# When the loads of B21, x and chunk 1 run, and in how many pieces, in a GEGLU feed-forward kernel (with the A22 copies split)

## The chip, the cores and the metric

One core of one Trainium2 chip. The metric is the device time of the kernel in microseconds (us). The kernel before the change takes 541.47 us, the median of three runs (540.5 to 542.04).

## The reference

```python
B, S, D, F = 1, 2048, 1024, 3584      # all in bfloat16
def reference(x, w_gate, w_up, w_down):
    return (gelu_tanh(x @ w_gate) * (x @ w_up)) @ w_down
```

## The kernel before

The kernel works on two halves of the sequence. In each half the gate and up projections are done in pairs of columns, and then the down projection in two groups, so there are four down groups in all (0 to 3). Every block product uses a scheme of seven products, M1 to M7, in place of eight; their operands are sums such as S1 to S4 (of the activations) and T1 to T4 (of the weights). T2 and T4 of the down projection are prepared in advance by VectorE ("staging", from pair 2 of the first half on), stored in device memory (`t_dram`), and loaded back for each group. SP issues nearly all loads and stores, in program order.

The loads of the down groups:

```python
def load_b21(n, q):                  # B21 of W_down, in 4 pieces of some 512 KB
    ...                              # pieces 0 to 2 into wd_sb buffers, the last into o_sb
    sp(nc.sync.dma_start(out=w[:, 0 : i1 - i0, :], in_=src))
    b21_tiles[(n, q)] = w

def t_down(grp, name, i0, i1):
    for i in range(i0, i1, 2):
        ...
        if name in ("t2", "t4"):
            src = t_dram[:, 0 if name == "t2" else 1, i : i + 2, :]
            sp(nc.sync.dma_start(out=t.bitcast(F32), in_=src))
        ...
```

One down group, cut to what the change touches:

```python
product("m5", VB, lsum(0), rsum("t1"), True, False, behind_m5)   # first of T2's loads in here
...
def behind_m6(i):
    ...
    if i == 4:
        for q in range(4):
            load_b21(n, q)
product("m6", QB, lsum(0), rsum("t2"), False, False, behind_m6, tail)
...
done("m6")                           # here the x loads (group 0) or chunk loads (group 1) are issued
product("m7", RB, lsum3, rsum("t3"), False, False, behind_m7, head)   # first of T4's loads in here
...
s_down(hT, grp, "a22", 0, NS)        # 7 copies on ScalarE, needed by M4
out22 = evacuate(VB, 1, 1)
done("m7")
store(out22)
product("m2", PB, h_block(0, 1), b21, False, True)
...
product("m3", QB, lsum(0), rsum("b22"), False, True, behind_m3)
...
product("m4", RB, lsum(1), rsum("t4"), False, True, behind_m4, tail)
```

The staging step, which the change does not touch but which the result turns on:

```python
def stage_step(n):                   # three subtractions for each block of W_down
    ...
    dve(nc.vector.tensor_tensor(out=t, in0=in0, in1=in1, op=ALU.subtract))
    if k > 0:
        sp(nc.sync.dma_start(out=t_dram[:, k - 1, i, :], in_=t.bitcast(F32)))
...
if h == 0 and pair >= PPG:           # PPG is 2: from pair 2 on; two steps in it, four in the next
    n = [min(max(4 * (pair - PPG + d) - 2, 0), NSTEP) for d in range(3)]
    steps = [lambda k=k: stage_step(k) for k in range(n[0], n[1])]
    new = range((n[1] + 2) // 3, (n[2] + 2) // 3)
```

The fill of the second half, during groups 0 and 1:

```python
def x_fill(k0, k1):
    src = x_dram[:, k0:k1, :]
    sp(nc.sync.dma_start(out=xT[0][:, k0:k1, :], in_=src))

def w_fill(c, j):
    if j == 0:
        new_chunk((nh, c))
    for k0 in range(0, KD, KH):      # two halves of each weight chunk
        load_w((nh, c), j, k0, k0 + KH)

then0["m6"] = [lambda k0=k0: x_fill(k0, k0 + WKP) for k0 in range(0, KD, WKP)]   # 4 loads
```

## Time and profile before

| | kernel before |
|---|---|
| time, median of 3 | 541.47 us (540.5 to 542.04) |
| the profiled run | 541.16 us, span 539.3 us |
| TensorE busy | 99% of the span |
| last matmul's start to the end of the span | 3.91 us |

The span is what the profile covers of one execution. TensorE is idle for 5.2 us of it (539.3 less 534.1), the start and the end included, so little is to be won by removing waits. The prediction shows the lines that locate one of them.

### The profile page before, as it was taken

To read this page: it belongs to the slowest core of one execution; us is meant where nothing else is said; L and a number is where in the kernel's file an instruction comes from. 1 tells how busy PE (TensorE), PEld (TensorE's weight loads), DVE (VectorE), ACT (ScalarE), POOL (GpSimd) and SP (SyncE) were. 2 spreads that over 40 slices of the span, in tenths; PEclk is the share of its full clock that TensorE was granted. 3 is DMA by queue.
4 is the path that set the end of the run, shared out by engine and by line. 5 is a ranking of instruction groups with operands and counts; after the bars stand their busy time and mean duration, and the time that the engine had idled before them with its cause. 6 is when DMAs were issued, how large, how long until landed. Compare 5 with 4: busy or idle time off the path is not lost.

```text
span 539.3 us, 7115 instructions
## 1 busy us (share of the span) xinstructions
PE 534.1 (99%) x2384; PEld 377.3 (70%) x2384; DVE 362.5 (67%) x478; ACT 263.2 (49%) x446; POOL 235.3 (44%) x208
## 2 busy tenths in 40 slices
PE   8999999999999999999999999999999999999997
PEld 3577776676776686767776767777777766866865
DVE  1968776887877997989574334444444469969951
ACT  2545555555555329117465555555555551552270
POOL 1069877777777000000056776666777730000000
PEclk9999999999999999999999999999999999999999
DMA  9954877695826977789950504042231466677846
GB/s 215 290 169 108 282 208 231 211 278 158 272 86 229 354 248 241 238 277 305 324 176 1 156 1 157 15 142 63 93 115 42 157 192 230 226 245 237 290 147 207
DMA packets 84836, 102.70 MB, mean 190 GB/s; under 512 B 18752, under 2 KB 66368, under 8 KB 84800
## 3 DMA queue, kind: packets, MB, share of 16 engines
q1 hardware_dynamic: 62400, 80.49, 47.1%
q10 hardware_dynamic: 22400, 21.76, 13.0%
q8 instruction: 19, 0.31, 0.2%
q14 instruction: 17, 0.14, 0.1%
HBM read 85.98 MB, written 12.58 MB: 183 GB/s over the span
## 4 chain that ended last, share of the span: by engine, by line
PE 97%; DMA 2%; ACT 0%; DVE 0%; issue 0%; ACTq 0%
PE bank L391 63%; PE bank L672 31%; PE bank L255 3%; DMA t_mem<-t_dram 1%; DMA w_mem<-in_x_dram 1%; PE bank L306 0%; ACT o_sb L725 0%; DVE xT L314 0%; ACTq L725 0%
## 5 line engine op out<-in xcount | busy, mean ns | idle before, releaser
L391 PE MATMUL bank<-t_mem,s_mem 128*128 128x512 f32 x1056 | 249.6, 394 | 0.0
L391 PEld LDWEIGHTS bank<-t_mem,s_mem 128*128 128x128 f32 x1056 | 198.1, 188 | 44.1 <-DVE bank L414 0.6
L362 POOL TENSOR_TENSOR s_mem<-w_mem 128x512 fp32r<-128x512 bf16 x102 | 117.4, 1171 | 200.5 <-DMA w_mem<-in_w_up_dram 102.7
L672 PE MATMUL bank<-t_mem,s_mem 128*128 128x512 f32 x544 | 127.4, 393 | 0.1
L279 DVE TENSOR_TENSOR hT<-w_mem,bank 128x512 bf16<-128x512 f32 x104 | 71.2, 687 | 82.9 <-PE bank L391 42.7
L672 PEld LDWEIGHTS bank<-t_mem,s_mem 128*128 128x128 f32 x544 | 102.1, 188 | 22.6 <-issue 0.5
L414 DVE TENSOR_TENSOR bank<-bank,m 128x512 f32<-128x512 f32 x108 | 69.9, 694 | 48.0 <-ACT m L439 44.0
L391 PE MATMUL bank<-xT,w_mem 128*128 128x512 bf16 x432 | 98.1, 380 | 0.0
L274 ACT ACTIVATE w_mem<-bank 128x512 f32<-128x512 f32 x104 | 61.8, 597 | 54.0 <-DVE bank L414 35.4
L391 PEld LDWEIGHTS <-w_mem 128*128 128x128 bf16 x432 | 40.2, 98 | 51.6 <-issue 6.8
L582 DVE TENSOR_TENSOR t_mem<-w_mem 128x1024 fp32r<-128x1024 bf16 x56 | 65.6, 1219 | 0.0
L362 POOL TENSOR_TENSOR s_mem<-w_mem,s_mem 128x512 fp32r<-128x512 bf16 x50 | 62.8, 1277 | 0.0
L362 POOL TENSOR_TENSOR s_mem<-s_mem,w_mem 128x512 fp32r<-128x512 f32 x50 | 57.4, 1167 | 0.0
L444 ACT COPY bank<-bank 128x512 f32<-128x512 f32 x54 | 30.8, 570 | 38.9 <-PE bank L391 37.2
L375 ACT CAST s_mem<-w_mem 128x512 fp32r<-128x512 bf16 x54 | 33.1, 615 | 31.7 <-PE bank L391 29.2
L647 DVE TENSOR_TENSOR s_mem<-hT 128x512 fp32r<-128x512 bf16 x52 | 34.2, 687 | 10.1 <-PE bank L672 9.4
L439 ACT COPY m<-bank 128x512 f32<-128x512 f32 x54 | 31.8, 589 | 18.4 <-PE bank L391 18.0
L672 PEld LDWEIGHTS <-hT 128*128 128x128 bf16 x224 | 21.2, 98 | 26.7 <-issue 2.1
L449 ACT COPY bank<-bank 128x512 f32<-128x512 f32 x54 | 30.7, 570 | 12.2 <-PE bank L391 12.2
L725 ACT CAST o_sb<-bank 128x512 bf16<-128x512 f32 x28 | 15.4, 585 | 40.0 <-PE bank L672 40.0
L607 DVE TENSOR_TENSOR o_sb<-wd_sb,o_sb 128x512 fp32r<-128x512 bf16 x28 | 30.4, 1085 | 0.5
L579 ACT CAST t_mem<-w_mem 128x1024 fp32r<-128x1024 bf16 x28 | 26.9, 1047 | 0.0
(45 smaller groups left out, 237.4 us busy)
## 6 DMA issues: line engine op xcount, KB each, us to landing
t_mem<-t_dram SPq DMA_DIRECT2D x56, 512.0 KB, 5.4
w_mem<-in_w_gate_dram ACTq DMA_DIRECT2D x10, 1024.0 KB, 5.5
w_mem<-in_w_up_dram ACTq DMA_DIRECT2D x10, 1024.0 KB, 8.2
wd_sb<-in_w_down_dram SPq DMA_DIRECT2D x28, 256.0 KB, 4.8
t_dram<-o_sb SPq DMA_DIRECT2D x28, 256.0 KB, 2.4
wd_sb<-in_w_down_dram SPq DMA_DIRECT2D x12, 512.0 KB, 8.1
w_mem<-in_w_down_dram SPq DMA_DIRECT2D x10, 512.0 KB, 7.5
w_mem<-in_w_down_dram SPq DMA_DIRECT2D x4, 1024.0 KB, 6.5
```

The costliest lines, as they stand in the source:

```text
L274: act(nc.scalar.activation(out=g_sb, in_=ps[:], func=ACT.Gelu_apprx_tanh))
L279: nc.vector.tensor_tensor(out=hT[:, fc, tb * TB : (tb + 1) * TB], in0=g_sb, in1=ps[:], op=ALU.mult,)
L362: pool(nc.gpsimd.tensor_tensor(out=t, in0=in0, in1=in1, op=op))
L375: act(nc.scalar.copy(out=t, in_=a(1, 1)))
L391: nc.tensor.matmul(banks[bank][:], lhsT=lhs[:, c, :], rhs=rhs[:, c, :], start=start and c == 0, stop=c == KH - 1, skip_group_check=True,)
L414: nc.vector.tensor_tensor(out=banks[dst][:], in0=banks[src][:], in1=m5[j][:], op=ALU.add)
L439: act(nc.scalar.copy(out=m5[j][:], in_=banks[V_[j]][:]))
L444: act(nc.scalar.copy(out=banks[RB[j]][:], in_=banks[QB[j]][:]))
L449: act(nc.scalar.copy(out=banks[QB[j]][:], in_=banks[P_[j]][:]))
L582: dve(nc.vector.tensor_tensor(out=t, in0=in0, in1=in1, op=ALU.subtract))
L647: dve(nc.vector.tensor_tensor(out=t, in0=in0, in1=in1, op=op))
L672: nc.tensor.matmul(banks[bset[u]][:], lhsT=lhs(i, u), rhs=rhs(i), start=start and i == 0, stop=stop and i == NS - 1, skip_group_check=True,)
```

## The change

Its intent: keep B21 from crowding the last loads of T2, move x out of the way of the T4 loads, issue fewer and larger loads, and let the output casts of M7 start before all seven A22 copies are done. The order of instructions on TensorE is the same in both kernels. (`t_loads`, kept in lines cut here, lists the T2 and T4 loads in order of issue, so `t_loads[-2]` is the sixth of the seven T2 loads.)

```diff
     def load_b21(n, q):
...
-        sp(nc.sync.dma_start(out=w[:, 0 : i1 - i0, :], in_=src))
+        load = nc.sync.dma_start(out=w[:, 0 : i1 - i0, :], in_=src)
+        if q == 0:
+            t2 = t_loads[-2]
+            tc.add_manual_dep(load.ins, t2.ins.name, SYNC_DEP, reason="rate")
+        sp(load)
...
-            if i == 4:
-                for q in range(4):
-                    load_b21(n, q)
-
+        for q in range(2):
+            load_b21(n, q)
+        done("b21")
+        for q in range(2, 4):
+            load_b21(n, q)
         product("m6", QB, lsum(0), rsum("t2"), False, False, behind_m6, tail)
...
-        s_down(hT, grp, "a22", 0, NS)
+        s_down(hT, grp, "a22", 0, NT2)
         out22 = evacuate(VB, 1, 1)
+        s_down(hT, grp, "a22", NT2, NS)
...
-            def x_fill(k0, k1):
-                src = x_dram[:, k0:k1, :]
-                sp(nc.sync.dma_start(out=xT[0][:, k0:k1, :], in_=src))
+            def x_fill():
+                sp(nc.sync.dma_start(out=xT[0][:], in_=x_dram[:]))
...
-                for k0 in range(0, KD, KH):
-                    load_w((nh, c), j, k0, k0 + KH)
+                n = 2 if c == 0 else 1
+                for k0 in range(0, KD, KD // n):
+                    load_w((nh, c), j, k0, k0 + KD // n)
...
-            then0["m6"] = [
-                lambda k0=k0: x_fill(k0, k0 + WKP) for k0 in range(0, KD, WKP)
-            ]
+            then0["b21"] = [x_fill]
```

More of the change, by code (lines that the diff above doesn't have):

```diff
@@ L64 @@
     KPQ = XQ // P
-    WKP = 2
     NWARM = 8
@@ L535 @@
     b21_tiles = {}
+    t_loads = []
     def load_b21(n, q):
@@ L576, in t_down @@
                 src = t_dram[:, 0 if name == "t2" else 1, i : i + 2, :]
-                sp(nc.sync.dma_start(out=t.bitcast(F32), in_=src))
+                t_loads.append(nc.sync.dma_start(out=t.bitcast(F32), in_=src))
+                sp(t_loads[-1])
             elif name == "b22":
```

## The prediction

> **What bounds the kernel now.** I read the page of the profile first: the engine shares, the chain that ended last, and the waits.
>
> ```profile
> span 539.3 us, 7115 instructions
> PE 534.1 (99%) x2384; PEld 377.3 (70%) x2384; DVE 362.5 (67%) x478; ACT 263.2 (49%) x446; POOL 235.3 (44%) x208
> PE 97%; DMA 2%; ACT 0%; DVE 0%; issue 0%; ACTq 0%
> PE bank L391 63%; PE bank L672 31%; PE bank L255 3%; DMA t_mem<-t_dram 1%; DMA w_mem<-in_x_dram 1%; PE bank L306 0%; ACT o_sb L725 0%; DVE xT L314 0%; ACTq L725 0%
> ```
>
> TensorE is busy for 99% of the span and carries 97% of the chain. Busy time alone does not prove a full pace, since matmuls overlap, so I checked the pace in the list of instructions in order of time. The chain, in order of time, has only two pieces of DMA. The first is the load of x before the first matmul, which this change leaves alone. The second is here:
>
> ```profile
> 183.78 34.90 PE bank L672 x156
> 218.68 0.02 issue
> 218.69 7.45 DMA t_mem<-t_dram
> 226.14 0.14 issue
> 226.28 45.80 PE bank L672 x203
> ```
>
> It looks like 7.45 us lost to a load. It is not: the chain follows back to what released a step, and TensorE worked through most of those 7.45 us. To see what the wait cost, take the matmuls of L672. They are the down projection: four groups (two halves of the sequence, two groups each, which I number 0 to 3), each of seven products of 28 matmuls, in the order M1, M5, M6, M7, M2, M3, M4. The load lies in M4 of group 0. M3 and M4 are 56 float32 matmuls in one row of the list; here are that row's four appearances, one of each group, and the weight loads of group 0:
>
> ```profile
> 214.64 13.49 PE L672 MATMUL bank<-t_mem,s_mem 128*128 128x512 f32 x56
> 258.98 13.09 PE L672 MATMUL bank<-t_mem,s_mem 128*128 128x512 f32 x56
> 478.78 13.09 PE L672 MATMUL bank<-t_mem,s_mem 128*128 128x512 f32 x56
> 522.73 13.09 PE L672 MATMUL bank<-t_mem,s_mem 128*128 128x512 f32 x56
> ...
> 214.61 11.11 PEld L672 LDWEIGHTS bank<-t_mem,s_mem 128*128 128x128 f32 x49
> 226.25 1.46 PEld L672 LDWEIGHTS bank<-t_mem,s_mem 128*128 128x128 f32 x7 [0.53 <-issue]
> ```
>
> Group 0 takes 13.49 us where each of the other three takes 13.09. The break stands after the 49th weight load, which is where M4 first needs the last piece of T4. So the stall costs 0.40 us, and no other group has it. The same check on M5, M6 and M7 (84 matmuls in one row of 19.44 us in group 1) shows no break. The gain that this change can find in the recorded execution is therefore 0.40 of 539.3 us, under 0.1%.
>
> **What the Trainium skill says.** "Perfetto Trace Analysis", section Identifying the Most-Contended Engine, warns that matmul busy time is a bad measure of closeness to the roof. Here the trace agrees only in part: 99% busy hid the 0.40 us stall, but the pace itself is even. "TensorE: Matmul & The Clock Gate", section Back-to-back issue gap, gives N/2.4 + 2.5 ns, about 216 ns for N = 512, as an isolated gap, and about 131 ns sustained beside weight loads. The trace does not show 131: M5 to M7 of group 1 run 84 matmuls from 233.84 to the next product at 253.12, 230 ns each. So there is no hidden faster pace to be released. "DMA: Bandwidth & Descriptors", section Issuing engines are not separate DMA queues, says that all transfers share the 16 engines and interleave. The trace agrees: the last T4 load of group 0 took 7.45 us from issue to landing, with x (1 MB) moving ahead of it, against 6.3, 6.6 and 6.4 us in groups 1 to 3. The same page, section Why small descriptors are slow, argues for longer runs; no number of the trace before isolates that.
>
> **The change, part by part.**
>
> The order of instructions on PE is the same in both kernels. No arithmetic is added or removed. ACT gains only split points, and SP issues five transfers fewer: x in one instead of four, and two large chunk loads instead of four. What moves is when transfers run.
>
> 1. x of the second half. Now its four loads stand behind all four B21 loads on SP:
>
> ```profile
> 204.65 0.37 SPq L546 DMA_DIRECT2D wd_sb<-in_w_down_dram  x1
> 205.12 0.45 SPq L546 DMA_DIRECT2D o_sb<-in_w_down_dram  x1
> 205.63 1.88 SPq L958 DMA_DIRECT2D xT<-x_dram  x4
> 207.62 2.00 SPq L577 DMA_DIRECT2D t_mem<-t_dram  x3
> ```
>
> The third B21 load waits until 204.65 for M7 to free its buffer (M7 of this group alone still reads four S3 blocks there), so x runs from 205.6 to 213.5 (the last issue at 207.1 plus 6.4), just ahead of the T4 loads. The changed kernel puts x behind the second B21 load. That one can issue near 199 (below), so x is through at an estimated 206: 1 MB at the 1.3 to 1.5 us per 512 KB that successive landings here show is some 3 us, behind 1 MB of B21. The first three T4 loads then start by about 207.2 instead of 207.62 and run alone. The last four keep their issue times, 215.95 to 218.69, since they wait for M3 to release B22. Without the backlog the last should take what groups 1 to 3 show, 6.3 to 6.6 us: landing near 225.2 instead of 226.14. M4 needs it 11.3 us into the 56 matmuls (49 times 231 ns), at 225.96. Slack: about 0.8 us. The whole 0.40 us stall goes. **Worth 0.40 us.**
>
> 2. B21 held back. The first B21 load waits until the sixth of seven T2 loads has landed. Before, B21 issued right behind the last T2 load and shared the engines with it. T2's last piece is also needed at the 49th matmul, of M5 and M6. From the list: M5 starts at 189.49, 233.84, 453.62 and 497.58; the last T2 loads issue at 193.55, 237.89, 457.68 and 501.64 and take 6.3, 6.9, 7.0 and 7.0 us. Landing is 10.4, 10.9, 11.1 and 11.1 us after the start, against 11.3 needed. It is in time in all four, by 0.2 to 0.9 us. So this part removes no recorded stall; it widens thin margins, by an estimated 1 to 1.5 us. An execution with a little more jitter may stall there now and not after. **Worth 0 in the trace, 0 to 0.3 us (a choice of mine) in other executions.**
>
> 3. Does B21 then come late for M2? In group 1 its first load moves from 238.27 to the landing of the sixth T2, 243.1 as now (237.0 plus 6.1), probably nearer 241.6. With the 3.7 us of an uncrowded B21 load it lands at 247, and the four at 1.45 us apart by 251. M2 starts at 253.12 and needs the last at about 258. Group 3 is alike. In groups 0 and 2 the first two have still more time. **Worth 0.**
>
> 4. Larger loads of chunk 1. The same bytes start at the same point, and the sums that read the chunk need both halves anyway. Landing at about 278 is long before pair 2 of the second half, which begins after two pairs of some 12.6 us from 271.9. **Worth 0.**
>
> 5. A22 copies split. Seven copies take 3.73 us (209.74 to 213.38), then the two output casts. After: three copies, casts, four copies. The casts can't start before VectorE's last additions at 212.1, so the outputs leave perhaps 1 us sooner and the last copy ends near 215.5. M4, which reads A22, starts at 221.1. **Worth 0.**
>
> Sum: 541.47 - 0.40 - about 0.1 = 541.0 us.
>
> **Rivals.**
> - The stall stays, because the last T4 load is slow by itself and not from x. For it: even in groups 1 to 3, where no x moves, it takes 6.3 to 6.6 us. Against it: 6.6 is soon enough. Time: 541.5.
> - Held B21, or x ahead of the third B21 load, makes M2 wait. For it: SP is one line, and a wait on it holds all that follows. Against it: the margins of 5 to 7 us in point 3; and in group 0 the third load still issues at 204.65 with M2 needing it at 212.2 (208.77 plus 16 matmuls of 216 ns). If one were missed by 2 us in each of two groups: 545.
> - T2 has been stalling unrecorded executions. For it: margins of 0.2 to 0.4 us in groups 1 to 3. Against it: the profiled execution took 541.16 us, inside the 540.5 to 542.04 of the others, so these can't hide much. If each of three groups stalled 0.3 us: 540.2.
>
> **Range and chances.** Working time of TensorE is untouched, so nothing but waits can move; the known one is 0.4 us and the three runs of before spread over 1.5 us. I take 540.0 to 542.1 for 8 in 10: the expected 541.0 with the spread of the runs on either side. A change of 2% is 10.8 us, 27 times the known stall, so faster gets 0.01. Slower needs several missed loads of microseconds each, and gets 0.01 also. Within 2%: 0.98.
>
> **What would show it.** Step 1 is right if the four rows of 56 matmuls all read 13.09 us, the DMA piece is gone from the chain at 218.7, and the last T4 load of group 0 takes at most 6.7 us. Step 2 is right if the last T2 loads take 5 to 6 us, not 6.3 to 7.0. Step 3 is wrong if a new break appears in the rows of M2, step 5 if one appears at the head of M4. The span should be 538.8 to 539.0. A new DMA piece in the chain, or a break in a row of M5 and M6, would make the prediction wrong.

## The result, and the profile after

| | before | after |
|---|---|---|
| time, median of 6 runs each in the same rounds | 541.86 us (540.5 to 542.04) | 542.26 us (541.13 to 543.51) |
| ratio of means, 95% interval | | 1.0011 (0.9992 to 1.0029) |
| profiled run, span | 541.16, 539.3 us | 542.15, 540.4 us |

All outputs are right. A ratio here is the mean time of one kernel's runs over that of the other's of the same rounds, so it is not quite the ratio of the medians quoted. By the measure of 2% the two kernels are the same, and the interval even includes 1. But the predicted gain of 0.4 to 0.5 us did not come; if anything there was a loss of that size.

These are lines of the page of the profile after. The first line is the span, the second the busy time of each engine, the third a DMA queue with its packets, MB and share of the engines (it matters below), and the last two the shares of the chain that ended last.

```profile
span 540.4 us, 7111 instructions
PE 534.3 (99%) x2384; PEld 377.4 (70%) x2384; DVE 363.9 (67%) x478; ACT 263.4 (49%) x446; POOL 233.8 (43%) x208
...
q14 instruction: 17, 0.14, 0.1%
...
PE 97%; DVE 1%; DMA 1%; ACT 0%; issue 0%; ACTq 0%
PE bank L390 62%; PE bank L678 33%; PE bank L254 3%; DVE o_sb L613 1%; DMA w_mem<-in_x_dram 1%; PE bank L305 0%; DVE hT L278 0%; ACT s_mem L374 0%; ACT o_sb L731 0%; ACT w_mem L273 0%; DVE xT L313 0%; ACTq L731 0%; ACTq L374 0%
```

The load of T4 has gone from the chain, as hoped. In its place VectorE has 1%, on a line (L613, the staging subtraction, L607 in the kernel before) that the change did not touch. The chain in order of time (start, length, what) shows where:

```profile
44.59 5.01 DVE o_sb L613
...
50.23 0.69 DVE hT L278
50.92 0.04 issue
50.97 133.97 PE bank L390 x596
184.93 87.89 PE bank L678 x392
```

This is pair 2 of the gate and up projection, 134 us before the first down group. The down projection itself is clean. These are the rows of M3 and M4 of groups 0 to 3 of the kernel after, in the list in order of time:

```profile
215.79 13.09 PE L678 MATMUL bank<-t_mem,s_mem 128*128 128x512 f32 x56
...
259.74 13.09 PE L678 MATMUL bank<-t_mem,s_mem 128*128 128x512 f32 x56
...
479.52 13.09 PE L678 MATMUL bank<-t_mem,s_mem 128*128 128x512 f32 x56
...
523.47 13.09 PE L678 MATMUL bank<-t_mem,s_mem 128*128 128x512 f32 x56
```

All four read 13.09, where group 0 of the kernel before read 13.49. To see where the time went, I cut both spans by the starts of the same matmuls (worked out from the trace):

```
                          before    after    difference, us
start to first matmul       4.85     4.49    -0.36   the load of x, untouched (warm-up left out)
pairs 0 to 2               63.09    64.61    +1.52   matmuls 0 to 300, untouched
rest of pairs, half 0     115.68   115.68     0
down group 0               44.35    43.95    -0.40   the T4 break
down group 1               43.95    43.95     0
half 1, gate and up       175.84   175.84     0
down groups 2 and 3        87.68    87.67     0
last matmul to the end      3.91     4.18    +0.27
sum                                          +1.01 (spans 539.35 and 540.36; rounding aside)
```

So three things are to be explained: a break of 1.5 us in a place that the change leaves alone, the 0.40 us that did go away, and 0.27 us at the end.

**The break in pair 2.** First the stretch from 44.7 to 47.5 us of the kernel before, in the list in order of time (start, length, engine, line, what; the bracket is idle time before it and its releaser):

```profile
44.74 2.72 POOL L362 TENSOR_TENSOR s_mem<-w_mem 128x512 fp32r<-128x512 bf16 x2
44.84 1.62 DVE L607 TENSOR_TENSOR o_sb<-wd_sb 128x512 fp32r<-128x512 bf16 x1
...
47.02 6.27 PE L391 MATMUL bank<-t_mem,s_mem 128*128 128x512 f32 x26
```

And the same stretch of the kernel after:

```profile
44.50 2.28 POOL L361 TENSOR_TENSOR s_mem<-w_mem 128x512 fp32r<-128x512 bf16 x2
44.59 5.00 DVE L613 TENSOR_TENSOR o_sb<-wd_sb 128x512 fp32r<-128x512 bf16 x1
...
46.72 2.32 POOL L361 TENSOR_TENSOR s_mem<-w_mem,s_mem 128x512 fp32r<-128x512 bf16 x2
...
46.77 3.10 PE L390 MATMUL bank<-t_mem,s_mem 128*128 128x512 f32 x12
...
50.23 0.68 DVE L278 TENSOR_TENSOR hT<-w_mem,bank 128x512 bf16<-128x512 f32 x1
...
50.97 2.33 PE L390 MATMUL bank<-t_mem,s_mem 128*128 128x512 f32 x9 [1.10 <-DVE hT L278]
```

The same subtraction, of two SBUF inputs, takes 1.62 us in one and 5.00 us in the other; its shortest in the trace is 0.68. In both it starts 0.1 us after a sum on GpSimd (POOL), in a run of such sums one behind the other. In the kernel before, GpSimd's two sums take 2.72 us, so GpSimd gave way once. In the kernel after, four sums on GpSimd go by at their own pace of some 1.15 us (44.50 to 49.04), and the subtraction ends 0.55 us after the last. The multiplication that writes hT stands behind it on VectorE, and TensorE stops: 12 matmuls, a wait, and "1.10 <-DVE hT L278". "SBUF — State Buffer", section Who interferes with whom, describes just this pair: a VectorE instruction with two SBUF inputs contends with a GpSimd instruction that reads SBUF, and one blocks the other for a whole instruction. The trace agrees that one waits and the other does not; that VectorE can stand back for four sums in a row, 4.3 us for a 0.68 us instruction, is what these lines add. No run takes the GpSimd sums away: that it is they that hold it is read from the lines and the page, not tested alone.

**The end.** Everything ends when the last store has landed. First the kernel before, then the kernel after: the last store's issue, and its time to landing.

```profile
L731 SPq DMA_DIRECT2D out_dram<-o_sb x1: 332/332/332, 536.5 to 536.5; - x1
...
DMA to landing us min/median/max: 1.8/1.8/1.8
```

```profile
L737 SPq DMA_DIRECT2D out_dram<-o_sb x1: 333/333/333, 537.3 to 537.3; - x1
...
DMA to landing us min/median/max: 2.3/2.3/2.3
```

The packets of the trace show one thing more about the store. A transfer of 8 KB on queue 14, which the page lists as one of instructions (17 packets, 0.14 MB), runs beside it; I call it the fetch. I give its start after the store's issue, its length, and the store's landing, from the packets of three profiles of each kernel (some of them taken in the experiments below; "shift" is explained there):

```
                 fetch starts   takes    store lands
before               0.55        0.39       1.80 us
before_again         0.35        0.72       2.00
before_shift         0.35        0.45       1.71
after                1.02        0.58       2.26
after_again          1.03        0.60       2.29
after_shift          1.04        0.76       2.59
```

In the kernel after, the fetch begins about 1.02 us after the issue instead of 0.35 to 0.55, when the store's own data is moving; 15 of the 16 engines are through with the store's packets by 1.34 us and the one left at 1.93. Its 8 packets (of 128) begin at 1.59 us, and the fetch ends at 1.60. In the kernel before all 16 are through by 1.34. The same 8 packets begin within 5 ns of the fetch's end in all seven profiles with the late fetch, which shows that it is the fetch that holds them up. Not all of the delay is paid: from the store's landing to the end of the span it takes 0.84 us here and 1.03 in the kernel before, which is why the cut shows 0.27 us and not 0.46.

### The profile page after: what moved, and what is told of

Its sections match the earlier page's. It is cut to its first block, busy times and chain, and to the rows that moved or that the text cites. A ratio compares the mean times of both kernels' runs of the same rounds, so it can differ in the third digit from the quotient of the medians.

```text
span 540.4 us, 7111 instructions
## 1 busy us (share of the span) xinstructions
PE 534.3 (99%) x2384; PEld 377.4 (70%) x2384; DVE 363.9 (67%) x478; ACT 263.4 (49%) x446; POOL 233.8 (43%) x208
## 4 chain that ended last, share of the span: by engine, by line
PE 97%; DVE 1%; DMA 1%; ACT 0%; issue 0%; ACTq 0%
PE bank L390 62%; PE bank L678 33%; PE bank L254 3%; DVE o_sb L613 1%; DMA w_mem<-in_x_dram 1%; PE bank L305 0%; DVE hT L278 0%; ACT s_mem L374 0%; ACT o_sb L731 0%; ACT w_mem L273 0%; DVE xT L313 0%; ACTq L731 0%; ACTq L374 0%
## 5 line engine op out<-in xcount | busy, mean ns | idle before, releaser
L278 DVE TENSOR_TENSOR hT<-w_mem,bank 128x512 bf16<-128x512 f32 x104 | 71.0, 686 | 82.9 <-PE bank L390 42.9
L361 POOL TENSOR_TENSOR s_mem<-w_mem,s_mem 128x512 fp32r<-128x512 bf16 x50 | 61.7, 1260 | 0.0
L613 DVE TENSOR_TENSOR o_sb<-wd_sb,o_sb 128x512 fp32r<-128x512 bf16 x28 | 29.9, 1066 | 0.5
```

Source lines behind the costliest of these rows:

```text
L278: nc.vector.tensor_tensor(out=hT[:, fc, tb * TB : (tb + 1) * TB], in0=g_sb, in1=ps[:], op=ALU.mult,)
L361: pool(nc.gpsimd.tensor_tensor(out=t, in0=in0, in1=in1, op=op))
```

## The experiments

My theory once the two traces were compared (theory A in the texts below) was this: the break in pair 2 is a race that either kernel can lose, while the stall in T4 is steady in the kernel before and the change did repair it. Theory B: the change itself costs time in the down projection. A rival to both: the change alone brings the break in pair 2. That the later landing of the last store belongs to the change became a theory (T) only with the second set of runs, split_shift and its companions.

### The two kernels again, unedited

> The changed kernel once more, unedited. Theory A (a race in the gate and up phase, which the change does not touch: VectorE's first staging subtraction stands against a streak of GpSimd sums and loses one or more turns): the runs scatter from about 540.8 (race won, no stall) to 543.5 (lost), the profile shows either a staging subtraction of about 5 us near 44.6 us and a break of about 1.2 us in TensorE, or neither; M3 and M4 of group 0 take 13.09 us either way. Ratio to before 0.998 to 1.003. Theory B (the change itself costs time in the down projection): the runs again average 0.5 us or more over before, and the profile has a new break after 184 us.

> The kernel before against itself: how far two equal kernels stand apart. Theory A: ratio 0.998 to 1.002, single runs from 540.5 to 543, the same race in the first staged pair visible in some execution (a staging subtraction over 2 us); the 0.4 us break in M4 of group 0 is there again (13.49 us for the 56 matmuls). Theory B: all its runs lie within 540.5 to 542.1 and it never shows the race.

Measured: after_again 542.73 us (542.38 to 543.61), ratio 1.0019 (0.9996 to 1.0042); before_again 541.63 (540.62 to 542.01), 0.9994 (0.9973 to 1.0016), beside 541.66 of the kernel before. In after_again the subtraction took 4.94 us again, in before_again it won again. Two of each are not enough to tell whether only the changed kernel loses. But the steady stall of theory A fell. before_again has no break in group 0, where 13.49 was expected, and after_again, with x moved ahead, has one in group 2. These are the rows of M3 and M4, first group 0 of before_again, then group 2 of after_again:

```profile
214.46 13.09 PE L672 MATMUL bank<-t_mem,s_mem 128*128 128x512 f32 x56
...
479.80 13.42 PE L678 MATMUL bank<-t_mem,s_mem 128*128 128x512 f32 x56
```

There the last T4 load took 7.4 us, with no x anywhere near it. Theory B had expected a new break after 184 us; this one is of the kind that the kernel before had. The means of this batch stand 1.03 us apart (541.76 and 542.79), more than the later store accounts for; whether the rest is chance or more lost races is not known.

### Both kernels without staging in pair 2 (after_shift, before_shift)

```diff
-n = [min(max(4 * (pair - PPG + d) - 2, 0), NSTEP) for d in range(3)]
+n = [0 if p <= PPG else min(4 * (p - PPG - 1) + min(max(p - PPG - 2, 0), 2), NSTEP)
+     for p in range(pair, pair + 3)]
-new = range((n[1] + 2) // 3, (n[2] + 2) // 3)
+new = range(max((n[1] + 2) // 3, 1), (n[2] + 2) // 3)
```

Pair 2 gets no subtraction, pair 3 four, pairs 4 and 5 five each. The contention is removed by giving VectorE no two-input work beside GpSimd's run of sums; no wait is taken away.

> The changed kernel with the staging subtractions begun one pair later (none in pair 2, four in pair 3, five in pairs 4 and 5), so that none stands against GpSimd's backlog. Theory A: no staging subtraction over 2 us, no break in TensorE near 50 us, runs narrow and at 540.6 to 541.2, about 1 us under the changed kernel's median of 542.26. Theory B: still 541.8 to 542.5 with the same spread.

> The kernel before with the same later staging. Theory A: runs narrow, 541.0 to 541.6, that is 0.4 us over the changed kernel with the same edit, and the 13.49 us for M3 and M4 of group 0 stays. Theory B: as the kernel before, 541.5 to 542, and about 0.5 us under the changed kernel with the edit.

Measured: after_shift 540.95 us (540.54 to 541.27), 0.9986 (0.9966 to 1.0006); before_shift 540.58 (540.35 to 540.84), 0.9979 (0.9958 to 0.9999). No subtraction takes longer than 1.82 us in either. These are the first subtractions of each block, as ns min/median/max, of the changed kernel, then of after_shift and before_shift:

```profile
L613 DVE TENSOR_TENSOR o_sb<-wd_sb x14: 676/1005/4997, 44.6 to 163.0; 128x512 fp32r<-128x512 bf16 x14
...
L613 DVE TENSOR_TENSOR o_sb<-wd_sb x14: 677/1002/1747, 47.6 to 161.4; 128x512 fp32r<-128x512 bf16 x14
...
L607 DVE TENSOR_TENSOR o_sb<-wd_sb x14: 677/886/1821, 48.2 to 162.0; 128x512 fp32r<-128x512 bf16 x14
```

Both medians fall by over 1 us (from 542.73 and 541.66 in the same batch) and the ranges shrink to 0.73 and 0.49 us, from 1.23 and 1.39 in after_again and before_again (six runs each). So the break in pair 2 is real, both kernels gain from its removal, and it is a large part of their spread, though not all (nowait_shift below still has a run of 542.86). before_shift missed its expectation under theory A: it stands under after_shift, not 0.4 us over it, and its row of M3 and M4 in group 0 reads 13.09. What is left between the two, 0.37 us, has the sign of theory B and is of the size of the later store. From here on the parts of the change were tried on the shifted kernels, where a few tenths can be seen.

### Three more looks at the kernel before (before_look1, before_look2, before_look3)

> The kernel before, one look, to catch it losing the race that both its profiles so far won. Theory R (its slower group of runs, 541.5 to 542.0, is the lost race): in about 7 of 10 looks a staging subtraction of about 5 us near 44.6 us, with a break of about 1.2 us in TensorE, and then a time of 541.5 or more; otherwise 540.3 to 541.2. Rival (the slower group is late T4 or T2 loads): never a staging subtraction over 2 us, and slow looks show 0.2 to 0.5 us breaks in the rows of 56 matmuls.

> As the first look: time and race go together (lost: about 5 us and 541.5 or more; won: about 1.6 us and 540.3 to 541.2).

> As the first look: time and race go together (lost: about 5 us and 541.5 or more; won: about 1.6 us and 540.3 to 541.2).

Measured: 541.5, 541.49 and 541.89 us, single runs of unknown state. All three lost the race. The first, in the list in order of time:

```profile
44.31 4.95 DVE L607 TENSOR_TENSOR o_sb<-wd_sb 128x512 fp32r<-128x512 bf16 x1
...
50.63 2.56 PE L391 MATMUL bank<-t_mem,s_mem 128*128 128x512 f32 x10 [1.05 <-DVE hT L279]
```

So it is not the change alone that brings the break: the kernel before loses the same way, in three of five profiles. The profile that the prediction was made from was one of the two lucky ones. Whether the changed kernel loses more often stays open: its profiles lost three of three, counting split_only below, but the runs that were not profiled cannot be sorted surely. In the kernel before, 12 of 57 timed runs lie at or under 541.0 and 33 between 541.3 and 542.1; of 12 runs of the changed kernel two lie near 541.15 and the rest at 542.15 or more.

### Which part moves the last store: undoing one or two parts (split_shift, merge_shift, nowait_shift, a22_shift)

All are on the shifted kernels. split_shift is after_shift with all large loads cut up again:

```diff
-                sp(nc.sync.dma_start(out=xT[0][:], in_=x_dram[:]))
+                for k0 in range(0, KD, 2):
+                    src = x_dram[:, k0 : k0 + 2, :]
+                    sp(nc.sync.dma_start(out=xT[0][:, k0 : k0 + 2, :], in_=src))
...
-                n = 2 if c == 0 else 1
+                n = 2
```

> The changed kernel with later staging, and x of the second half back in four transfers and chunk 1 back in halves: SP has as many transfers as in the kernel before; waits, places and the A22 split as changed. Theory T (the 0.4 us by which the changed kernel with later staging, 540.97, still stands over the kernel before with the same, 540.58, lies in the very last store: an instruction fetch of 8 KB runs 1.0 us after that store's issue, on top of its data, where in the kernel before it runs 0.35 to 0.55 us after and is out of the way; where the fetch falls depends on the number of instructions): the last store lands 1.7 to 2.0 us after its issue, runs at 540.4 to 540.8. Theory W (the B21 wait or the moved x costs it): last store still 2.3 to 2.6 us or a break elsewhere, runs at 540.8 to 541.2.

merge_shift is before_shift with only the loads merged, at their old places:

```diff
-            then0["m6"] = [
-                lambda k0=k0: x_fill(k0, k0 + WKP) for k0 in range(0, KD, WKP)
-            ]
+            then0["m6"] = [lambda: x_fill(0, KD)]
...
-                for k0 in range(0, KD, KH):
-                    load_w((nh, c), j, k0, k0 + KH)
+                n = 2 if c == 0 else 1
+                for k0 in range(0, KD, KD // n):
+                    load_w((nh, c), j, k0, k0 + KD // n)
```

> The kernel before with later staging, and only x and chunk 1 merged into larger transfers at their old places: five SP transfers fewer, no B21 wait, no moved x, no A22 split. Theory T: last store 2.2 to 2.6 us, runs at 540.8 to 541.2. Theory W: last store 1.7 to 2.0 us, runs at 540.4 to 540.8.

nowait_shift is after_shift without the wait of B21 for T2:

```diff
-        if q == 0:
-            t2 = t_loads[-2]
-            tc.add_manual_dep(load.ins, t2.ins.name, SYNC_DEP, reason="rate")
```

> The changed kernel with later staging, without the B21 wait alone: the last T2 loads go back to 6.3 to 7.0 us from 5.7 to 6.4, no break in M5 and M6 follows. Theory T: runs 540.8 to 541.2 as with the wait, unless the count of instructions moved. Theory W with the wait as cause: 540.4 to 540.8.

a22_shift is after_shift with the A22 copies in one block again:

```diff
-        s_down(hT, grp, "a22", 0, NT2)
+        s_down(hT, grp, "a22", 0, NS)
         out22 = evacuate(VB, 1, 1)
-        s_down(hT, grp, "a22", NT2, NS)
```

> The changed kernel with later staging, with the A22 copies in one piece again. Prediction's step 5: no difference, runs 540.8 to 541.2, no break at the head of M4. Rival: the split is what delays the end (its order moves the last casts), runs 540.4 to 540.8.

Measured, beside the kernel before (541.78 us):

| | median (range), us | ratio (95%) | fetch after issue | store lands |
|---|---|---|---|---|
| split_shift | 540.40 (540.27 to 540.79) | 0.9975 (0.9963 to 0.9988) | 0.36 us | 1.74 us |
| merge_shift | 540.98 (540.82 to 541.82) | 0.9990 (0.9977 to 1.0002) | 1.03 | 2.60 |
| nowait_shift | 541.14 (540.7 to 542.86) | 0.9987 (0.9974 to 1.0001) | 1.02 | 2.33 |
| a22_shift | 541.37 (540.62 to 541.63) | 0.9990 (0.9978 to 1.0003) | 1.03 | 2.53 |

Merging the loads is enough to bring the later store, and cutting them up is enough to undo it; the wait of B21 and the split of A22 have nothing to do with it. The profiled run of nowait_shift is its slowest (542.86): there VectorE waits 1.9 us for a load of W_down in the next pairs, and TensorE stops for 1.4 us, a break of the first half again and not one that the removed wait explains. In group 1 of that profile the last T2 load takes 7.17 us and the group 44.09 us instead of 43.95, a stall of 0.14 us where none was expected, and which the B21 wait may guard against. But it is no sure guard: a22_shift has the wait, yet its last T2 loads in groups 1 and 2 took 7.12 and 7.21 us, and it lost 0.16 us in M5 and M6 of group 2. That same profile also shows the T4 stall without x near it: its last T4 load of group 2 took 7.23 us, and the row of M3 and M4 13.27.

### Cut-up loads without the shift (split_only)

The edit of split_shift, made to the changed kernel as it stands.

> The changed kernel with x in four transfers and chunk 1 in halves again, staging left where it was: what remains of the change is the B21 wait, the earlier place of x and the A22 split. If the tail and the race are all there is: last store 1.7 to 2.0 us; runs in two groups as the kernel before has them, near 540.4 (race won) and 541.5 to 542.0 (lost); ratio to before 0.998 to 1.001. If the kept parts cost or gain anything of their own: outside that.

Measured: 542.06 us (541.34 to 543.76), 1.0009 (0.9989 to 1.003), beside 541.81 of the kernel before. The store lands after 1.80 us, with the fetch at 0.54, as expected; the race was lost in the profile (4.99 us); group 1 lost 0.27 us to a last T4 load of 7.33; and none of the six runs fell into the lower of the two groups that I expected. With the race in play, 0.5 us at the end can't be read from six runs. It is why the shifted kernels were needed.

### Size of the transfers, or something about the program (pad_shift, xsplit_shift, csplit_shift)

A large transfer long before the end can hardly slow the last store by itself, but merging also makes the program of SP shorter: the trace of after_shift holds 381 instructions on SP, waits included, against 385 in before_shift. pad_shift keeps all large transfers of after_shift and adds five loads of 2 KB each, into a buffer that nobody reads (387). xsplit_shift cuts up x alone (383), csplit_shift the chunk loads alone (385).

```diff
+            pads = const_pool.tile([P, 5, 8], BF16, name="pads")
+            def pad(k):
+                sp(nc.sync.dma_start(out=pads[:, k, :], in_=x_dram[:, k, 0:8]))
+            then0["m3"] = [lambda: [pad(k) for k in range(5)]]
```

> The changed kernel with later staging, its large transfers kept, and five tiny loads of 16 bytes per partition added on SP during M3 of group 0, into a tile nobody reads: SP's program is as long as in the kernel before. Theory L (the length of SP's program decides where the last instruction fetch falls): fetch 0.35 to 0.55 us after the last store's issue, that store lands in 1.7 to 2.0 us, runs at 540.3 to 540.8. Rival S (it is the larger transfers themselves): fetch still at 1.0 us, 2.2 to 2.6 us, runs at 540.8 to 541.4.

> The changed kernel with later staging and x alone back in four transfers, chunk 1 merged: three instructions fewer between this and the changed one. Theory L: the fetch stands at one of the two places, or between them, and the last store and the time follow it (0.35 to 0.55 us: 1.7 to 2.0 us and 540.3 to 540.8; about 1.0 us: 2.2 to 2.6 us and 540.8 to 541.4). Rival S with x as cause: 540.3 to 540.8; with the chunk as cause: 540.8 to 541.4, both without the fetch moving.

> The changed kernel with later staging and chunk 1 alone back in halves, x in one transfer: two more instructions than the changed one. Theory L: as for the other, the last store and the time follow the place of the fetch. Rival S: the opposite of what x alone shows, without the fetch moving.

Measured, beside the kernel before (541.73 us):

| | SP, ScalarE instructions | median (range), us | ratio (95%) | fetch | store lands |
|---|---|---|---|---|---|
| pad_shift | 387, 707 | 540.40 (540.06 to 540.89) | 0.9974 (0.9952 to 0.9996) | 0.35 us | 1.80 us |
| xsplit_shift | 383, 706 | 541.24 (540.67 to 541.47) | 0.9987 (0.9967 to 1.0007) | 1.04 | 2.48 |
| csplit_shift | 385, 707 | 540.20 (539.93 to 540.44) | 0.9970 (0.9950 to 0.9990) | 0.36 | 1.71 |

pad_shift decides between size and program: with the large transfers kept, five tiny loads alone bring the fetch back to 0.35 us and the time to 540.40. So it is not the size of a transfer. A count of instructions does fit. Waits are instructions too, and with them counted all 17 profiles fall apart cleanly: the fetch is late in the seven with 378 to 383 instructions on SP and 706 on ScalarE, and early in the ten with 385 to 387 on SP and 707 on ScalarE (chunk loads in halves, or the pads, give ScalarE one wait more). Transfers alone do not sort them: SP issues 227 in xsplit_shift, late, and 226 in csplit_shift, early. The two counts moved together, so whether the fetch is of SP's program or of ScalarE's is not tested. "Runtime: NRT & Kernel Launch", section Instruction fetch mechanics, says that each engine's sequencer fetches its own instructions by DMA in blocks while it runs, at a cost that is "mostly hidden"; here the fetch is 8 KB, and where it falls on the data of the last store it is not hidden.

csplit_shift is the best version found: all of the change but the merged chunk loads, and staging that begins one pair later. The chain of its profile in order of time has no break left after the first 24 us, only the ordinary pace of TensorE:

```profile
23.56 159.82 PE bank L390 x712
183.38 87.89 PE bank L678 x392
271.27 175.84 PE bank L390 x784
447.11 87.91 PE bank L678 x392
```

Its ratio, 0.9970 (0.9950 to 0.9990), lies below 1 for the whole interval. It is 1.5 us below the median of the kernel before in the same rounds, and 2.5 us below that of after_again in another batch. At 0.3% it still counts as the same by the measure of 2%.

## Why the prediction was right or wrong

**Right: the class.** Within 2%, for the reason given: TensorE's work is untouched and only waits can move.

**Step 1, x ahead of the T4 loads, "Worth 0.40 us": failed.** The overlap that it rests on was not there. It read the last T4 load as slow "with x (1 MB) moving ahead of it", but by its own lines the last of x landed at 213.5, and this load was issued at 218.69, 5.2 us later; so it does not show the sharing of the DMA engines for which the prediction cites it. x ran into the first three T4 loads only, and the last of these had landed by 217.45. What the step said of the loads held in part. x issued at 200.56 us (199 predicted, on a clock that by then ran some 1.1 us later) and landed 7.6 us on, at 208.2, later than the estimated 206. The first three T4 loads did get faster: the first and third took 3.9 and 5.8 us instead of 7.2 and 8.5. The last took 6.9 us, where at most 6.7 was to show the step right, landing 10.96 us into the 56 matmuls instead of 11.50, and the row reads 13.09. The last T4 load takes 5.8 to 7.5 us in either kernel, and a break follows where it needs over about 7.1: 7.45 in group 0 of the profile before (0.40 us lost) and 7.17 in that of before_look2 (0.12), but also 7.38 in group 2 of after_again, 7.33 in group 1 of split_only and 7.23 in group 2 of a22_shift, with no x near. With x in its old place two of seven profiles have a break in group 0, with x moved none of ten: too few to say that x adds nothing. But before_look3, whose first three T4 loads took longest of all (8.8 to 10.0 us), had none. I took one stall of one execution for a property of the kernel. My own first rival, that the last load is slow by itself, fits the runs better, and I set it aside because three groups of a single profile happened to be in time. What makes the load late is not known.

**Step 2, B21 held back, "Worth 0 in the trace, 0 to 0.3 us … in other executions": right.** The last T2 loads took 6.0, 6.0, 5.8 and 5.7 us instead of 6.3, 6.9, 7.0 and 7.0. That is about the predicted 5 to 6. No break had been there to remove, and those seen in other runs were 0.1 to 0.2 us. But the wider margin is not assured: with the same wait, last T2 loads still took up to 7.21 us in a22_shift and 7.25 in pad_shift, and lost some 0.2 us there. The margins were also thinner than the 0.2 us of the prediction: in pad_shift that load landed 11.31 us into M5 and M6 and cost 0.21 us, so it was needed at 11.1 us, not at 11.3.

**Step 3, B21 in time for M2, and step 5, the split of A22, worth 0 each: right.** No row of M2 and none of M4 shows a new break; groups 0 to 3 take 43.95, 43.95, 43.95 and 43.72 us (the last to the start of its last matmul). The A22 split was not seen to gain either.

**Step 4, larger loads of chunk 1, "Worth 0": right on the loads, wrong on the kernel.** Nothing waits for chunk 1, as argued. But merging loads, x and chunk 1 together, changes the program, and with it the place of the last instruction fetch: the last store lands 2.26 to 2.60 us after its issue instead of 1.71 to 2.00, and the time grows by 0.4 to 0.6 us where the race is out of the way (before_shift 540.58 to after_shift 540.95; split_shift 540.40 to merge_shift 540.98). csplit_shift to xsplit_shift is 1.04 us, of which their profiles show 0.83 after the last matmul. "Worth 0" should have been a loss, and no step of the prediction looked at the end of the span at all. Of the two merges, that of the chunk is the one to undo: csplit_shift has the early fetch and xsplit_shift has not.

**The sum and the range.** "541.47 - 0.40 - about 0.1" began from a median of three that stood low: the same kernel gave medians of 541.63 to 541.86 in six sets of 6 to 11 runs (the first holds those three). Strike the gain of 0.40, add about 0.45 for the late store, an estimate from the runs above, and the sum from 541.8 is 542.25, where 542.26 was measured. The agreement to 0.01 is luck, given the spread of the race and an estimate made afterwards. The range of 540.0 to 542.1 took its upper end from the three runs known, while the kernel itself reaches 543 to 544 in some runs. A break that the profile did not hold, the lost race in pair 2 (a wait of 1.05 us on TensorE), was in three of its five profiles. I read that as 1.5 us of "spread" and did not ask what it was.

**What stays open.** What decides who wins in pair 2, and whether the changed kernel loses more often. What makes a last T4 load late, and whether x has a small part in it. Whether SP's or ScalarE's program places the last fetch.

## What to carry to other kernels

Before a stall of some tenths of a microsecond is called the thing to fix, see it in a second profile of the same kernel; a spread of 1.5 us over runs of one kernel is itself a finding with a cause, and here it was the larger one, worth over 1 us. When a change touches only transfers, compare also the part after the last matmul, since even the length of a program can move what happens there. Where TensorE waits for what stands behind a two-input VectorE instruction, as here in pair 2, try moving that instruction away from a dense run of GpSimd sums.

## What the Trainium skill lacked or had wrong

- "SBUF — State Buffer" says that the second of the two blocks until the first finishes. The runs show that it may block for several instructions of the other engine: VectorE's 0.68 us subtraction took 4.94 to 5.00 us beside four GpSimd sums of some 1.15 us, and 1.62 us at the same place in another execution. The page doesn't say who gets the turn when one ends and the other already waits.
- "Runtime: NRT & Kernel Launch" gives instruction blocks of 16 KiB and a cost that is mostly hidden. Packets of 16 KiB do appear on queue 8 of these profiles, but the last fetch is one of 8 KB on queue 14. It takes 0.39 to 0.76 us, and where it starts 1.02 to 1.04 us after the last store's issue the store lands after 2.26 to 2.60 us instead of 1.71 to 2.00.
- No page says that such a fetch can fall on the data of the last store, or that a few instructions more or fewer can move it there: with 378 to 383 instructions on SP and 706 on ScalarE it was late, with 385 to 387 and 707 early.
- No page gives the spread of a load's landing in a busy kernel: the last 512 KB of T4, issued at the same point of each group, landed after 5.8 to 7.5 us.
